# Scratch layout of q and k, pacing of the matrix comparison, and a bound in three steps, in a two-layer attention and Fourier kernel

## The chip, the cores and the metric

The kernel runs on one core of one Trainium2 chip. The metric is the device time of one execution in microseconds; the kernel before takes 2665.07 us (median of 3 runs, 2664.98 to 2665.43). Engines are called as the profile calls them: PE (matmul; PEld is its weight load), DVE (vector), ACT (scalar), POOL (GpSimd), SP (issues transfers). POOL and SP both start DMA transfers, each in the order of its own program.

## The reference

Two layers, each an attention block and a Fourier block on x of 2048 rows and 640 columns, 32 heads of 20 columns:

```
x = x + attention(layernorm(x))     # q, k, v = x @ wqkv;  softmax(q k^T / sqrt(20)) v;  @ wo
x = x + fourier(layernorm(x))       # a = x @ hid_re^T, b = x @ hid_im^T;  seq_re @ a - seq_im @ b
x = x + attention(layernorm(x))
x = x + fourier(layernorm(x))
```

The four matrices of the Fourier block are inputs. The kernel uses their mirror symmetry, and so compares their halves with each other once, in layer 0; a general path stands behind the comparison for matrices that aren't symmetric.

## The kernel before

**One layer.** A prologue normalizes and transposes x, and makes the first chunks of q and k and half of v. Then comes the attention, then the projection with wo, then the Fourier part. Most of the time is the attention: 8 groups of 4 heads, in a group 4 blocks of 512 queries (`qb`), in a block 16 chunks of 128 keys (`kc`): 512 steps a layer, numbered n. In a step `scores` (L469) makes four matmuls `psc<-stq,stk` and two exponentials `e<-psc` on ACT, and `values` (L480) the four matmuls `acc<-e,v` of a step or two earlier. After the last chunk of a block `finish` (L491) takes the sum `acc` out of PSUM with DVE (transpose `of`, division, transpose back `ot`, split `oh`), and POOL writes it out in eight transfers `o<-oh`, `o<-ot`. This finish of one block stands at kc 1 of the next.

**Exact halves.** A number f32 is split into a rounded part (high) and the rest (low). A score needs high times high, high times low, low times high. So the tile `stk` has, for each head, 60 rows of k (high, low, high) and `stq` 60 rows of q (high, high, low), and two rows of shift below them. `keep` (L208) writes both parts of a chunk of 128 columns of q or k and 512 rows of x to scratch in DRAM, `scr`, with a POOL transfer; `kload` (L433) and `qload` (L443) read them from there with SP transfers: for each head one of 40 rows and one of 20 rows, and for q one of the two rows of shift.

**Work beside the attention.** The other chunks of q, k and the second half of v are made during the attention, on PE, in the gaps of ACT (`work`, L347). For a chunk of 512 rows there are two pieces of matmuls `pqk<-xt,wqk`, two steps apart, then `keep` on DVE (`hl` twice, `sq`), two steps later the norms (`pn` on PE, `top` on DVE), and after four of these the weights of the next chunk are split on DVE (`wqk`, two instructions, `weights` L201). They all use one PSUM bank, `fill`: the next piece can start on PE only when `top` has read that bank and `wqk` is there. For v, `v<-pv` on DVE empties the bank. `due` (L541) says when a piece is due, `fill(n)` (L557) issues it, after the scores of its step. Work of this kind lasts to about step 350 in both layers.

**The comparison** (`Check`, L640, layer 0 only). 42 loads of 1 MB (two transfers `cq<-in_nat_seq_dram` of 512 KB) or less, and two small ones; POOL issues them, into two tiles that every load uses again. Behind each load stand four empty tasks and then the comparisons of it: the largest element (`ctop`), edges (`cedge`, small instructions), three or four pairs of a 128x512 subtraction (L688) and a reduction (L684). All tasks together are one list of 469. `begin(n)` (L574), ahead of the scores of step n, takes tasks from the list as long as fewer than 469 n / 490 are done; a load is held back when n modulo 64 is under 6 or over 54, that is around the change of a group. So the list can fall behind, and is then caught up within one step.

**The bound.** The scores of a group are shifted by a bound on them, from the norms. `bound(g + 1)` (L403) is called at kc 0 of the last block of group g: three small reductions on DVE, a power on POOL (L406), its product on DVE (L407), a copy to a row `sh` of 512 (L409), and an SP transfer to DRAM (L410), from where `qload` reads the two rows of shift. `sh`, the two tiles `of` and `ot` of `finish`, and `zeros` share one buffer (tag `ofsh`): the next to be written in it waits until the one before is read, by a transfer too.

**Loads around the change of a group.** In the last block of a group SP gets: at kc 0 the shift row, at kc 1 `kload` of the first half for heads 0 and 1 of the next group, at kc 4 its `qload`, at kc 9 and 11 two more `kload`; the last one comes at kc 0 of the new group and is used from its kc 8. There are five tiles for k and two pairs for q.

Of the kernel before, what the change touches and what calls it, by code (L numbers as in the profile page):

```python
# [5 lines left out]
F32 = mybir.dt.float32  # L6
# [28 lines left out]
def mha_fnet_kernel(ctx, tc, x_in, wqk, wv, wo, seq, hid, nat_seq, nat_hid, out):  # L35
# [123 lines left out]
    class Qkv:  # L159
        def __init__(s, L, src):  # L160
            s.L, s.src = L, src
            s.xn, s.xt, s.rs, s.v = {}, {}, {}, {}
            s.scr = {qk: dr.tile([2, D, S], F32, name=f"scr{qk}_{L}") for qk in "qk"}
            s.shift = {n: dr.tile([H, 2, c], F32, name=f"shift{n}_{L}") for n, c in (("b", 512), ("m", S))}
            s.n = 0
            s.made, s.raw = set(), {}
# [41 lines left out]
        def keep(s, p, c, tb, vector, room):  # L208

            hl = room("hl", [2, 512], F32R, "hl")  # L210
            sq = room("sq", [512], BF, "sq")
            h = hl[:, 0].bitcast(F32)
            if vector:
                split(hl[:, 0], hl[:, 1], p, vector)
                V.tensor_tensor(sq, h, h, op=OP.mult)
# [6 lines left out]
            G.dma_start(d[c * 128:(c + 1) * 128, :, tb * 512:(tb + 1) * 512], hl.bitcast(F32))  # L222
            return sq
# [38 lines left out]
        def prologue(s, vals, xt, fill, room, att):  # L262
# [36 lines left out]
            for tb in range(NB):  # L299
# [23 lines left out]
                if tb == 0:  # L323
                    att.qload(0, 0, None)
                elif tb == 1:
                    s.fetch(ND + 1)
                    for j in range(2):
                        att.kload(0, 0, j)
                elif tb == 2:
                    s.w1 = s.weights(s.fill("w", [2, ND, 128], F32R, "wqk"), ND + 1, True)  # L330
                    s.fetch(1)
                elif tb == NB - 1:
                    att.zeros(room)
                    s.bound(0, room)
                    att.qshift(0, 0)
                    for j in range(2):
                        att.kload(0, 1, j)
# [65 lines left out]
        def bound(s, g, room):  # L403

            r = s.bounds()
            G.tensor_tensor(r[:H, 3:4], r[:H, 2:3], half[:H, 0:1], op=OP.pow)  # L406
            V.tensor_scalar(r[:H, 3:4], r[:H, 3:4], -1.02, None, op0=OP.mult)  # L407
            sh = room("ofsh", [512], F32R, "sh")
            V.tensor_copy(sh[:H], r[:H, 3:4].to_broadcast([H, 512]))  # L409
            nc.sync.dma_start(s.shift["b"][4 * g:4 * g + 4, 0], sh[4 * g:4 * g + 4].bitcast(F32))  # L410

    class Attention:
# [17 lines left out]
        def kload(s, g, f, j):  # L433
# [3 lines left out]
            for i in range(2):  # L437
                r = slice((4 * g + 2 * j + i) * DH, (4 * g + 2 * j + i + 1) * DH)
                d = t[64 * i:64 * i + 60].bitcast(F32)
                nc.sync.dma_start(d[0:40], s.a.scr["k"][0:2, r, cols])  # L440
                nc.sync.dma_start(d[40:60], s.a.scr["k"][0, r, cols])

        def qload(s, g, qb, shift):  # L443
# [3 lines left out]
            for j in range(2):  # L447
                s.q[g, qb, j] = tiles[j]
                for i in range(2):
                    h = 4 * g + 2 * j + i  # L450
                    r = slice(h * DH, (h + 1) * DH)
                    d = tiles[j][64 * i:64 * i + 62].bitcast(F32)
                    nc.sync.dma_start(d[0:40], s.a.scr["q"][0:1, r, cols].to_broadcast([2, DH, 512]))
                    nc.sync.dma_start(d[40:60], s.a.scr["q"][1, r, cols])
                    if shift is not None:
# [78 lines left out]
        def run(s, done, project, check):  # L534

            work, tasks, later = s.a.work(), s.a.vweights(1, s.a.fill, pause=[lambda: None] * 2), list(check)
            s.work, s.blocks, s.after, s.rest, s.more = True, 0, None, 0, False

# [18 lines left out]
            def fill(n):  # L557
# [16 lines left out]
            def begin(n, g, qb, kc):  # L574
                if qb == NB - 1 and kc == 0 and g + 1 < H // 4:
                    c0, c1 = (g + 1) * 80 // 128, ((g + 2) * 80 - 1) // 128
                    need(n, c0, c1, ND + c0, ND + c1, *(["v"] if g + 1 >= 4 else []))
                    s.a.bound(g + 1, s.room)
                while later and (len(check) - len(later)) * 490 < n * len(check):
                    task = later.pop(0)  # L580
                    if isinstance(task, tuple):

                        if n % 64 < 6 or n % 64 > 54:
                            later.insert(0, task)
                            break
                        task = task[1]
                    task()

# [4 lines left out]

            s.sweep("b", begin, fill)
            assert not s.work and not later and not tasks, (len(later), len(tasks))
# [44 lines left out]
    class Check:  # L640
# [20 lines left out]
        def tasks(s):  # L661
# [6 lines left out]
            for i in range(2 * s.MID):  # L668
                out += [("load", lambda i=i: s.load(i))] + 4 * [lambda: None] + s.compare(i)
            for m in range(2):  # L670
                out += [("load", lambda m=m: s.middle(m))] + 4 * [lambda: None] + s.compare_middle(m)
            return out + [s.end, s.sum]
# [647 lines left out]
```

## Time and profile before

| | |
|---|---|
| time, median of 3 runs | 2665.07 us |
| the profiled execution: its time | 2668.6 us |
| its span, first to last instruction | 2666.7 us |
| mean granted clock of PE | 0.983 |
| busy: PE, ACT, DVE, POOL | 95%, 80%, 37%, 20% |
| exponentials `e<-psc`, ACT | 2048 in 1937.3 us of busy time |
| matmuls `acc<-e,v` / `psc<-stq,stk` | 1065.5 / 823.4 us of busy time |
| DMA, mean over the span | 99 GB/s |

The page gives for each engine the time in which it was busy, and for each group of instructions its number, the time of all, the mean of one, and how long the engine stood idle ahead of them and for whom. Matmuls overlap and their ends are modelled, so PE is called busy in times in which it could take more; whether the attention loses time is seen better from ACT, which has two exponentials to do in each step, and from the waits of PE. The two layers run the same program but for the comparison, which layer 0 alone has: a stage can be compared with itself.

### The profile page before, as it was taken

Reading aid. Unit: us, or ns where it says so; the run is one execution under the profiler, and the core shown is the slowest. Engines: PE = TensorE matmul, PEld = TensorE weight load, DVE = VectorE, ACT = ScalarE, POOL = GpSimd, SP = SyncE. Lnnn points to the kernel's source line nnn. Section 1 sums busy time; section 2 is a strip of 40 time slices with the busy share of each in tenths; the row PEclk is TensorE's granted clock in tenths of the full one; section 3 lists DMA queues with packets and bytes.
Section 4 is the critical chain, followed back from the end, with each engine's and each line's share of the span. In section 5 each row is a group of like instructions: output and inputs, shape, how many; then the busy total and the mean of one; then the engine's idle time right before and its main releaser. Section 6 shows DMA issues by size and latency. Waiting matters only on the chain. (4 is left out here: it accounts for less than half of the span.)

```text
span 2666.7 us, 43675 instructions
## 1 busy us (share of the span) xinstructions
PE 2542.7 (95%) x16350; PEld 1169.8 (44%) x16350; DVE 978.2 (37%) x2049; ACT 2136.3 (80%) x2429; POOL 525.0 (20%) x1062
## 2 busy tenths in 40 slices
PE   7999898989999999999969999999999999999997
PEld 6633343433333322228758444444433333222586
DVE  5354434435444444225553233211331211221265
ACT  5587697978899999994334888999889999999642
POOL 2122112112222212213241111111111111111133
PEclk9999999999999999999989999999999999999999
DMA  4333222223323322317263222111222111222264
GB/s 158 114 109 115 96 88 93 75 102 107 118 90 104 93 90 84 117 39 258 98 215 106 80 91 80 54 41 43 74 71 73 48 66 52 69 71 89 85 227 179
DMA packets 121820, 263.97 MB, mean 99 GB/s; under 512 B 24984, under 2 KB 49336, under 8 KB 121580
## 3 DMA queue, kind: packets, MB, share of 16 engines
q1 hardware_dynamic: 80684, 150.55, 16.7%
q0 software_dynamic: 40896, 110.34, 12.9%
q8 instruction: 137, 2.24, 0.4%
q14 instruction: 103, 0.84, 0.1%
HBM read 176.60 MB, written 84.16 MB: 98 GB/s over the span
## 5 line engine op out<-in xcount | busy, mean ns | idle before, releaser
L478 ACT ACTIVATE e<-psc 128x1024 f32<-128x1024 f32 x2048 | 1937.3, 1193 | 211.4 <-PE psc L475 175.8
L486 PE MATMUL acc<-e,v 128*32 128x512 f32 x8192 | 1065.5, 604 | 6.7 <-DVE of L493 6.6
L475 PE MATMUL psc<-stq,stk 62*128 62x512 f32 x4096 | 823.4, 465 | 8.0 <-DMA stk<-scrk 4.9
L475 PEld LDWEIGHTS psc<-stq,stk 62*128 62x128 f32 x4096 | 342.3, 184 | 850.9 <-ACT e L478 794.1
L486 PEld LDWEIGHTS acc<-e,v 128*32 128x32 f32 x8192 | 187.8, 108 | 369.2 <-issue 337.8
L126 PE MATMUL pqk<-xt,wqk 128*128 128x512 f32 x1200 | 317.5, 408 | 23.7 <-DVE top L228 13.4
L507 POOL DMA_DIRECT2D o<-oh x256 | 131.2, 518 | 803.5 <-DVE oh L502 774.9
L126 PEld LDWEIGHTS pqk<-xt,wqk 128*128 128x128 f32 x1200 | 217.0, 190 | 111.7 <-issue 39.6
L111 DVE CAST hl<-pqk 128x512 fp32r<-128x512 f32 x64 | 44.2, 691 | 517.9 <-PE pqk L126 516.7
L493 DVE STREAM_TRANSPOSE of<-acc 128x512 f32<-128x512 f32 x64 | 45.8, 716 | 376.5 <-PE acc L486 376.4
L126 PE MATMUL pv<-wv,xt 128*128 128x320 f32 x960 | 163.7, 322 | 11.7 <-DVE v L258 7.6
L126 PEld LDWEIGHTS pv<-wv,xt 128*128 128x128 f32 x960 | 144.6, 193 | 38.8 <-issue 24.6
L507 POOL DMA_DIRECT2D o<-ot x256 | 127.9, 506 | 5.4 <-DMA cq<-in_nat_seq_dram 4.6
L222 POOL DMA_DIRECT2D scrq<-hl x40 | 29.9, 748 | 440.7 <-DVE hl L114 311.4
L119 PE MATMUL py<-wo,o 128*128 128x320 f32 x320 | 100.9, 315 | 13.5 <-DVE xr L867 7.1
L684 DVE TENSOR_REDUCE far<-cq 128x1 f32<-128x512 f32 (+5 forms) x169 | 98.6, 584 | 5.7
L121 PE MATMUL py<-wo,o 128*128 128x320 f32 x320 | 100.2, 313 | 0.0
L120 PE MATMUL py<-wo,o 128*128 128x320 f32 x320 | 100.2, 313 | 0.0
L688 DVE TENSOR_TENSOR cq<-cq 128x512 f32<-128x512 f32 (+4 forms) x166 | 96.6, 582 | 7.4 <-DMA cq<-in_nat_seq_dram 7.3
L222 POOL DMA_DIRECT2D scrk<-hl x40 | 29.6, 740 | 352.6 <-DVE hl L114 337.4
L684 DVE TENSOR_REDUCE ctop<-cq 128x1 f32<-128x512 f32 (+2 forms) x44 | 27.4, 622 | 169.2 <-DMA cq<-in_nat_seq_dram 123.4
L258 DVE COPY v<-pv 128x320 f32<-128x320 f32 x32 | 15.7, 489 | 185.5 <-PE pv L126 185.5
(191 smaller groups left out, 1764.5 us busy)
## 6 DMA issues: line engine op xcount, KB each, us to landing
cq<-in_nat_seq_dram POOLq DMA_DIRECT2D x64, 512.0 KB, 5.4
scrq<-hl POOLq DMA_DIRECT2D x40, 512.0 KB, 3.2
scrk<-hl POOLq DMA_DIRECT2D x40, 512.0 KB, 5.0
stq<-scrq SPq DMA_DIRECT2D x256, 80.0 KB
stk<-scrk SPq DMA_DIRECT2D x128, 160.0 KB
o<-o SPq DMA_DIRECT2D x16, 1280.0 KB
stq<-scrq SPq DMA_DIRECT2D x256, 40.0 KB
stk<-scrk SPq DMA_DIRECT2D x128, 80.0 KB
```

What stands on the lines that cost most here:

```text
L119: PE.matmul(out_ap, ah, bh, start=start, stop=False)
L120: PE.matmul(out_ap, ah, bl, start=False, stop=False)
L121: PE.matmul(out_ap, al, bh, start=False, stop=stop)
L126: yield lambda i=i, j=j, k=k: PE.matmul(out_ap, a[i], b[j], start=dc == 0 and k == 0, stop=dc == ND - 1 and k == 2)
L222: G.dma_start(d[c * 128:(c + 1) * 128, :, tb * 512:(tb + 1) * 512], hl.bitcast(F32))
L475: PE.matmul(p[:, i], s.k[g, kc // 8, j][r, kc % 8 * 128:(kc % 8 + 1) * 128], s.q[g, qb, j][r], start=True, stop=True)
L478: A.activation(e, p, AF.Exp, scale=SCALE)
L486: PE.matmul(s.acc[32 * j:32 * j + 32], s.a.v[kc][:, v0:v0 + 32], s.e[n, j // 2][:, j % 2], start=kc == 0, stop=kc == NT - 1, skip_group_ch ...
L493: V.transpose(t0.rearrange("p b c -> p (b c)"), s.acc)
L507: G.dma_start(s.o[k, h * DH:(h + 1) * DH, qb * 512:(qb + 1) * 512], hl[k][32 * j:32 * j + DH])
L684: V.tensor_reduce(to, x, op=OP.max, axis=AX.X, apply_absolute_value=True)
L688: V.tensor_tensor(y, x, y, op=op)
```

## The change

There are four parts.

1. The scratch of q and k is laid out as column, part, row of x (`[D, 2, S]` in place of `[2, D, S]`): the high and low parts of a column follow each other. `kload` then reads 40 rows with one step between them, in the order high, low of each column, and `qload` reads each high row twice in a row; the order of rows in `stk` and `stq` changes in the same way in both, and the sum over them is the same.
2. The comparison has a function of its own, `compare(n)`, which is called after `fill(n)`, so behind the scores and the piece of work of its step. It takes two tasks a step at most, and after a load no task for five steps. The four empty tasks are gone (293 tasks in the list), and so is the ban around the change of a group.
3. `bound` is a generator in three steps: reductions and power at kc 0, product and copy to `sh` at kc 3, the transfer at kc 5.
4. `qload` for the next group is at kc 7 of the last block in place of kc 4; within a group it stays at kc 4.

```
-            s.scr = {qk: dr.tile([2, D, S], F32, name=f"scr{qk}_{L}") for qk in "qk"}
+            s.scr = {qk: dr.tile([D, 2, S], F32, name=f"scr{qk}_{L}") for qk in "qk"}
...
-            d = s.scr["qk"[k]].rearrange("j d t -> d j t")
-            G.dma_start(d[c * 128:(c + 1) * 128, :, tb * 512:(tb + 1) * 512], hl.bitcast(F32))
+            G.dma_start(s.scr["qk"[k]][c * 128:(c + 1) * 128, :, tb * 512:(tb + 1) * 512], hl.bitcast(F32))
...
             G.tensor_tensor(r[:H, 3:4], r[:H, 2:3], half[:H, 0:1], op=OP.pow)
+            yield
             V.tensor_scalar(r[:H, 3:4], r[:H, 3:4], -1.02, None, op0=OP.mult)
             sh = room("ofsh", [512], F32R, "sh")
             V.tensor_copy(sh[:H], r[:H, 3:4].to_broadcast([H, 512]))
+            yield
             nc.sync.dma_start(s.shift["b"][4 * g:4 * g + 4, 0], sh[4 * g:4 * g + 4].bitcast(F32))
+            yield
...
-                nc.sync.dma_start(d[0:40], s.a.scr["k"][0:2, r, cols])
-                nc.sync.dma_start(d[40:60], s.a.scr["k"][0, r, cols])
+                k = s.a.scr["k"][r, :, cols]
+                nc.sync.dma_start(d[0:40], k.rearrange("r j t -> (r j) t"))
+                nc.sync.dma_start(d[40:60], k[:, 0])
...
-                    nc.sync.dma_start(d[0:40], s.a.scr["q"][0:1, r, cols].to_broadcast([2, DH, 512]))
-                    nc.sync.dma_start(d[40:60], s.a.scr["q"][1, r, cols])
+                    q = s.a.scr["q"][r, :, cols]
+                    nc.sync.dma_start(d[0:40], q[:, 0:1].to_broadcast([DH, 2, 512]))
+                    nc.sync.dma_start(d[40:60], q[:, 1])
...
-                if kc == 4 and not (last and g == H // 4 - 1):
+                if kc == (7 if last else 4) and not (last and g == H // 4 - 1):
...
+            def compare(n):
+                for _ in range(2):
+                    if not later or n < s.landed or (len(check) - len(later)) * 490 >= n * len(check):
+                        break
+                    task = later.pop(0)
+                    if isinstance(task, tuple):
+                        s.landed = n + 5
+                        task = task[1]
+                    task()
...
-                    s.a.bound(g + 1, s.room)
-                while later and (len(check) - len(later)) * 490 < n * len(check):
-                    task = later.pop(0)
-                    if isinstance(task, tuple):
-                        if n % 64 < 6 or n % 64 > 54:
-                            later.insert(0, task)
-                            break
-                        task = task[1]
-                    task()
+                    s.shift = s.a.bound(g + 1, s.room)
+                if qb == NB - 1 and kc in (0, 3, 5) and g + 1 < H // 4:
+                    next(s.shift)
...
-                out += [("load", lambda i=i: s.load(i))] + 4 * [lambda: None] + s.compare(i)
+                out += [("load", lambda i=i: s.load(i))] + s.compare(i)
```

Three places in the order of instructions. The first is DVE around step 70 of layer 0, where the work beside the attention ends a chunk: `top<-pn` empties the bank, `wqk` are the weights of the next chunk, the rows on `cq` are comparisons of load 5. Before:

```order
L727 COPY cq<-cq 128x2
L688 TENSOR_TENSOR cq<-cq 128x512
L684 TENSOR_REDUCE far<-cq 128x1
L688 TENSOR_TENSOR cq<-cq 128x512
L684 TENSOR_REDUCE far<-cq 128x1
L228 TENSOR_REDUCE top<-pn 32x1
L111 CAST wqk<-wraw 128x640
L114 TENSOR_TENSOR wqk<-wraw,wqk 128x640
L688 TENSOR_TENSOR cq<-cq 128x512
```

and in the changed kernel:

```order
L697 TENSOR_REDUCE far<-cedge 128x1
L739 TENSOR_SCALAR cq<-cq 128x2
L740 COPY cq<-cq 128x2
L227 TENSOR_REDUCE top<-pn 32x1
L111 CAST wqk<-wraw 128x640
L114 TENSOR_TENSOR wqk<-wraw,wqk 128x640
L701 TENSOR_TENSOR cq<-cq 128x512
L697 TENSOR_REDUCE far<-cq 128x1
L701 TENSOR_TENSOR cq<-cq 128x512
```

Two pairs of subtraction and reduction have moved from ahead of `top` and `wqk` to behind them.

The second place is POOL at the change from group 0 to group 1, steps 49 to 68: the writes of the finished block (`o_95`), writes to scratch (`scrk_92`) and loads for the comparison (`cq`). Before:

```order
L507 DMA o_95<-ot 20x512 x4
L679 DMA cq<-in_nat_seq_dram 128x2x512 x2
L222 DMA scrk_92<-hl 128x2x512 x3
L507 DMA o_95<-oh 20x512 x4
L507 DMA o_95<-ot 20x512 x4
L222 DMA scrk_92<-hl 128x2x512
L679 DMA cq<-in_nat_seq_dram 128x2x512 x4
```

and now:

```order
L511 DMA o_95<-ot 20x512 x4
L221 DMA scrk_92<-hl 256x1x512
L692 DMA cq<-in_nat_seq_dram 128x2x512 x2
L221 DMA scrk_92<-hl 256x1x512 x2
L692 DMA cq<-in_nat_seq_dram 128x2x512 x2
L511 DMA o_95<-oh 20x512 x4
L511 DMA o_95<-ot 20x512 x4
L221 DMA scrk_92<-hl 256x1x512
```

Load 5 (the second `cq` row) has moved from behind the next block's writes and step 68's scratch write to ahead of the former, at step 64.

The third place is DVE in the last block of group 0, steps 48 to 52. Before, `sh` of the bound stands ahead of the finish of the block before (from `of<-acc` on):

```order
L400 TENSOR_TENSOR bound<-bound 32x1
L407 TENSOR_SCALAR bound<-bound 32x1
L409 CAST sh<-bound 32x512
L688 TENSOR_TENSOR cq<-cq 128x512
L684 TENSOR_REDUCE far<-cq 128x1
L688 TENSOR_TENSOR cq<-cq 128x256
L684 TENSOR_REDUCE far<-cq 128x1
L493 STREAM_TRANSPOSE of<-acc 128x512
```

Now it stands behind that finish (whose last instructions are the first three rows) and behind a `keep` (`hl`, `sq`), and ahead of the `top` of that `keep`:

```order
L504 STREAM_TRANSPOSE ot<-on 128x512
L506 CAST oh<-ot 128x512
L507 TENSOR_TENSOR ot<-ot,oh 128x512
L111 CAST hl<-pqk 128x512
L114 TENSOR_TENSOR hl<-pqk,hl 128x512
L215 TENSOR_TENSOR sq<-hl 128x512
L407 TENSOR_SCALAR bound<-bound 32x1
L409 CAST sh<-bound 32x512
L701 TENSOR_TENSOR cq<-cq 128x256
L697 TENSOR_REDUCE far<-cq 128x1
L227 TENSOR_REDUCE top<-pn 32x1
```

`sh` takes the buffer that `ot` held, so it has moved from a place where the transfers of an earlier block were the last readers to one where the four `o<-ot` of this finish are.

More of the change, by code (lines that the diff above doesn't have):

```diff
@@ L333, in prologue @@
                     att.zeros(room)
-                    s.bound(0, room)
+                    list(s.bound(0, room))
                     att.qshift(0, 0)
@@ L536, in run @@
             work, tasks, later = s.a.work(), s.a.vweights(1, s.a.fill, pause=[lambda: None] * 2), list(check)
-            s.work, s.blocks, s.after, s.rest, s.more = True, 0, None, 0, False
+            s.work, s.blocks, s.after, s.rest, s.more, s.landed = True, 0, None, 0, False, 0
             marks = ((0, 0), (44, 16), (236, 80), (364, 96), (512, 120))
@@ L592, in begin, with between @@
                     f()
-            s.sweep("b", begin, fill)
+            def between(n):
+                more = fill(n)
+                compare(n)
+                return more
+            s.sweep("b", begin, between)
             assert not s.work and not later and not tasks, (len(later), len(tasks))
@@ L668, in tasks @@
             for i in range(2 * s.MID):
-                out += [("load", lambda i=i: s.load(i))] + 4 * [lambda: None] + s.compare(i)
+                out += [("load", lambda i=i: s.load(i))] + s.compare(i)
             for m in range(2):
-                out += [("load", lambda m=m: s.middle(m))] + 4 * [lambda: None] + s.compare_middle(m)
+                out += [("load", lambda m=m: s.middle(m))] + s.compare_middle(m)
             return out + [s.end, s.sum]
```

## The prediction

> **What bounds the kernel now.** The two layers run the same attention, but only layer 0 compares matrices, so I lay them beside each other. The first view sums ACT's exponentials over the stretch of each group of 64 steps (stretch in us from the span's start, its length, ACT's busy time and number, granted clock of PE, DMA share, GB/s). Layer 0, then layer 1:
>
> ```profile
> 251.79:403.91 152.12, 123.88 (x129) 0.97 0.29 95
> ...
> 963.18:1080.42 117.24, 117.24 (x129) 1.00 0.29 86
> ...
> sum 1100.57, ACT 969.28; mean ACT 121.16
> ```
> ```profile
> 1604.76:1744.75 139.99, 123.84 (x128) 1.00 0.21 66
> ...
> 2270.51:2387.76 117.25, 117.25 (x129) 1.00 0.22 68
> ...
> sum 1048.12, ACT 968.02; mean ACT 121.00
> ```
>
> Layer 0 takes 1100.57 - 1048.12 = 52.45 us longer for the same exponentials. Group 6, in which comparisons run but no other work, takes 117.24 against 117.25 us: ACT is busy throughout, a step costs 117.25 / 64 = 1.83 us, and the comparison is free. Group 1, with work on PE beside it, takes 12.1 us longer. So the comparison costs only where something on PE waits for DVE. The next view gives what PE waited for (sum, times, longest), in the attention of layer 0 and then of layer 1:
>
> ```profile
> PE pqk L126 <- DVE top L228: 12.7, 3, 9.9
> PE pqk L126 <- DVE wqk L111: 9.2, 2, 8.5
> PE pv L126 <- DVE v L258: 7.6, 1, 7.6
> PE psc L475 <- DMA stk<-scrk: 4.9, 2, 3.7
> PE pn L227 <- DVE sq L215: 4.9, 3, 3.0
> PE acc L486 <- DVE of L493: 4.8, 11, 1.1
> PE psc L475 <- ACT e L478: 1.5, 3, 0.7
> ```
> ```profile
> PE acc L486 <- DVE of L493: 1.8, 10, 0.2
> PE psc L475 <- ACT e L478: 1.5, 3, 0.7
> PE pqk L126 <- DVE wqk L111: 0.8, 1, 0.8
> PE pqk L126 <- DVE top L228: 0.7, 2, 0.4
> PE pn L227 <- DVE sq L215: 0.5, 2, 0.3
> ```
>
> They sum to 45.6 and 5.3 us, a difference of 40.3. Layer 0 has four long waits (9.9, 8.5, 7.6, 3.7) and one of 3.0; nothing in layer 1 is over 0.8. The other 12 us are the clock. The stretches of layer 0's attention at half the granted clock that follow these waits, with PE's busy time first (the column ahead of 1.00 or 0.50 is POOL):
>
> ```profile
> 237.73:241.14 3.41, 3.41 (x15) 1.00 (x16) 3.34 (x7) 1.94 (x2) 0.00 (x0) 0.50 0.52 185
> 271.86:282.10 10.24, 4.54 (x12) 2.82 (x12) 8.56 (x22) 0.00 (x0) 1.33 (x2) 0.50 0.12 37
> 432.29:442.53 10.24, 6.50 (x28) 3.20 (x28) 6.45 (x12) 1.91 (x2) 1.43 (x2) 0.50 0.12 42
> 568.82:579.06 10.24, 4.22 (x10) 2.98 (x12) 6.06 (x16) 0.00 (x0) 1.42 (x2) 0.50 0.27 89
> 722.42:729.25 6.83, 6.63 (x25) 1.68 (x25) 5.29 (x9) 3.12 (x4) 0.72 (x1) 0.50 0.17 61
> ```
>
> PE works 25.3 us in them, which at full clock would take half: 12.6 us. With 40.3 that makes 52.9, near the measured 52.45. Layer 0's excess is explained, and it is all that the change can take back.
>
> **The pacing.** The list has 469 tasks over 490 steps, 0.96 a step. A load held back from about step 61 to step 70 leaves nine tasks due at once: the load, four empty ones, and four comparisons of that very load. So the comparison waits for a transfer issued in the same step, and `top` and `wqk` stand behind it (first place of the order). The timeline shows it:
>
> ```profile
> 264.90 1.45 POOL L679 DMA_DIRECT2D cq<-in_nat_seq_dram  x2
> 271.79 0.69 DVE L684 TENSOR_REDUCE ctop<-cq 128x1 f32<-128x512 f32 x1 [7.33 <-DMA cq<-in_nat_seq_dram]
> 273.79 0.69 DVE L688 TENSOR_TENSOR cq<-cq 128x512 f32<-128x512 f32 x1
> 274.51 0.69 DVE L684 TENSOR_REDUCE far<-cq 128x1 f32<-128x512 f32 x1
> 275.12 0.68 DVE L688 TENSOR_TENSOR cq<-cq 128x512 f32<-128x512 f32 x1
> 277.56 3.78 PE L126 MATMUL pqk<-xt,wqk 128*128 128x512 f32 x8 [8.47 <-DVE wqk L111]
> ```
>
> DVE sits 7.33 us on the transfer, then does comparisons, a pair every 1.33 us; PE waits 8.47 us for `wqk`. The two lines of pacing give the same pattern wherever the ban ends: steps 70, 134, 198, 262, 326, which are the places of layer 0's excess.
>
> In the changed kernel no comparison comes sooner than five steps after its load: 5 x 1.83 = 9.2 us at least, against 271.79 - 264.90 = 6.9 us here. The four long waits should go with their clock. What remains I count from the new order. At step 208 a pair now stands between a `keep` and the next `wqk`, at the place where layer 1 already waits 0.8 us, so its 1.33 us are exposed: **1.3 us**. Around step 84 the order holds about what it held: of the shorter `top` waits I keep **0.8**. The waits of `acc` for `of` come from pairs just ahead of a finish; a pair or two still stands there in a dozen blocks: I keep 4.8 - 1.8 = **3.0**.
>
> **The bound: an added wait.** `sh` at kc 3 now takes the buffer of `ot`, whose four writes have only been issued (third place). In layer 1, first change of group, from DVE, POOL and PE, and the landing of all `o<-ot` writes:
>
> ```profile
> 1567.06 0.41 DVE L409 CAST sh<-bound 32x512 fp32r<-32x512 f32 x1
> ...
> 1571.52 0.72 DVE L493 STREAM_TRANSPOSE of<-acc 128x512 f32<-128x512 f32 x1 [4.05 <-PE acc L486]
> ...
> 1577.79 0.68 DVE L228 TENSOR_REDUCE top<-pn 32x1 f32<-32x512 f32 x1 [0.47 <-PE pn L227]
> ```
> ```profile
> 1577.41 2.00 POOL L507 DMA_DIRECT2D o<-ot  x4
> ```
> ```profile
> 1580.86 2.12 PE L126 MATMUL pqk<-xt,wqk 128*128 128x512 f32 x8
> ```
> ```profile
> DMA to landing us min/median/max: 1.8/3.5/7.5
> ```
>
> The last of the four starts at 1577.41 + 1.5 = 1578.9; with the median it lands at 1582.4. DVE holds at `sh` until then, needs 0.41 us for it, and `top` follows with 0.68: 1583.5. PE wants the bank at 1580.86, so it waits **2.7 us**; in layer 0 a pair on 256 of the 512 columns stands ahead of `top` too, between half and all of 1.33, say 0.85: **3.55 us**. With the shortest and longest landing these would be 1.0 to 6.7 in layer 1; I take the median. At the other changes of group nothing on PE stands behind `sh` before it is done: after group 1 and 2 the work is v, whose next bank is needed four and more steps later, then there is no piece until kc 12. Before, the same buffer was waited for at kc 0, fifteen steps after its writes; that costs nothing and goes.
>
> **The loads.** While only 40-row loads of k run (700 to 703 us), SP's queue takes 12.6% of 16 DMA engines, two of them; in the 0.3 us of a 20-row load beside one, 61.8%, ten:
>
> ```profile
> q1 hardware_dynamic: 39, 0.16, 12.6%
> ```
> ```profile
> q1 hardware_dynamic: 13, 0.05, 61.8%
> ```
>
> The order prints the old 40-row source with a dimension ahead (`40x1x1024`) and the new one plain (`40x1024`), as the 20-row load always was. So I expect the 160 KB to spread over ten engines. The two late `stk` (4.9 us above) go with it; in layer 1 nobody waits for these loads, so nothing more is gained there. What this covers is the later `qload`: `sh` is done 1582.8 - 1571.5 = 11.3 us, 6.2 steps, after the finish of kc 1 began (the row of `of`), so at kc 8, and q and one `kload` have 8 steps, 14.6 us, left. A write to scratch is now issued as 256 rows; were its 748 ns doubled, POOL, which stands idle 440 us ahead of those writes, would hide it:
>
> ```profile
> L222 POOL DMA_DIRECT2D scrq<-hl x40 | 29.9, 748 | 440.7 <-DVE hl L114 311.4
> ```
>
> The Trainium skill, "DMA: Bandwidth & Descriptors", section "Why a DMA increments its semaphore by 16 and not by 1", says that a transfer runs on the largest number of engines up to 16 that divides the outermost dimension on both sides. By that the old 40-row loads get 2 (the 12.6% agrees), the new ones of k and of q 10; for q, whose printed shape does not change, no run here shows it. With that rule q is as quick as k and the sum below stands; without it the third case below becomes likelier.
>
> **Sum.** Left over: 1.3 + 0.8 + 3.0 + 2.7 + 3.55 = 11.4 us. Gain: 52.45 - 11.4 = 41.0. The profiled execution took 2668.6 us (span 2666.7), so 2627.6; the median of the runs shown is 3.5 us lower, and I forecast **2624 us**, with 2616 to 2633 for other landings of `ot`, a half-clock stretch after the 3.55 us (half of 3.41: 1.7), and other waits of `acc`.
>
> **Rivals.**
>
> *Nothing new waits:* the `ot` writes land early, since the two crowded engines are freed, and the pairs stay hidden. Then only some of the 52.45 stay: 2612 to 2616. For it: landings as short as 1.8. Against: the median, and the 1.3 us at step 208.
>
> *The pairs crowd DVE:* two tasks in a step are 2.7 us against 1.83 to 2.5 of a step, and in the new order some 13 `keep` cycles have a pair or more before the next piece. If each exposes one, 13 x 1.33 = 17 us more: 2641. Against: layer 0's short waits already hold such cycles at a fraction of that.
>
> *The loads come late (slower):* if 40-row loads stay on two engines, q and k can miss the first step of a group. The place is SP's queue in the last block:
>
> ```profile
> 677.08 0.61 SPq L453 DMA_DIRECT2D stq<-scrq  x1
> ...
> 693.28 0.22 SPq L456 DMA_DIRECT2D stq<-shiftb  x1
> ```
>
> The twelve issues of q took 16.4 us there. With them 14.6 us are overrun; four issues of k (2.4, at 0.61) and 3.0 us for the 160 KB that the 12.6% row moved in its window make 7.2 us late, at 14 changes of group 101 us: some 2725. It decides against the change from 41 / 14 = 2.9 us on. If the loads spread, the sixteen issues alone take at most 16 x 0.61 = 9.8 us, and with 3.5 us to land they fit, with 1.3 us to spare.
>
> **How the numbers follow.** Forecast 0.70; nothing new waits 0.09; pairs crowd DVE 0.14; loads late 0.07, of which 0.04 lose more than the rest gains. The range from 2613 to 2640 holds the first three nearly whole. A measurement of this kernel can tell about 0.2%, 5 us, from no change. Faster by more: 0.94; within: 0.02; slower: 0.04.
>
> **What would show it.** Right: layer 0's attention some 9 us above layer 1's, which is 1 to 3 us above 1048; no wait of PE over 4 us in it; waits of `pqk` for `top` near step 54 in both layers, with DVE standing at `sh` for the DMA `o<-ot`; SP's queue at more than half of 16 engines under k loads; no half clock but perhaps after step 54. Wrong: PE waiting for `stq` or `stk` at the first step of a group, or DVE idle for `cq` ahead of a `keep`'s `top`.

## The result, and the profile after

The changed kernel takes 2623.84 us, the median of four runs (2622.28 to 2624.82), beside 2665.03 (2664.98 to 2665.43): a ratio of 0.9845, 95% interval 0.9828 to 0.9862. Against this 2624 was forecast. The profiled execution took 2624.82 us, with a span of 2623.0 against 2666.7. The span is cut at the exponentials:

| stretch, us | before | after | less |
|---|---|---|---|
| attention of layer 0 | 1100.57 | 1057.59 | 42.98 |
| between the two attentions | 259.22 | 257.84 | 1.38 |
| attention of layer 1 | 1048.12 | 1049.08 | -0.96 |
| ahead of the first and behind the second | 258.8 | 258.5 | 0.3 |

The gain lies in layer 0's attention, as forecast; the 1.38 us between the attentions was not. The groups of 64 steps, by the view that sums ACT's exponentials over each (stretch, its length, ACT's busy time and number, PE's granted clock, DMA share, GB/s), layer 0 and then layer 1:

```profile
249.10:390.54 141.44, 124.10 (x128) 1.00 0.34 109
...
sum 1057.59, ACT 968.51; mean ACT 121.06
```
```profile
1561.11:1701.10 139.99, 123.85 (x128) 1.00 0.21 66
...
sum 1049.08, ACT 968.02; mean ACT 121.00
```

Group 1 was 12.1 us longer in layer 0 than in layer 1, and is now 1.45 longer. Its granted clock was 0.97 and is 1.00. What PE still waits for (sum, times, longest), in the attention of layer 0 and of layer 1:

```profile
PE acc L490 <- DVE of L497: 6.6, 12, 2.3
PE pqk L126 <- DVE top L227: 3.5, 3, 2.8
```
```profile
PE acc L490 <- DVE of L497: 1.8, 10, 0.2
PE pqk L126 <- DVE top L227: 1.7, 3, 1.0
```

The waits of 9.9, 8.5 and 7.6 us for `top`, `wqk` and `v` are gone, and so is `stk`. The longest left is 2.8 us. Of the five stretches at half clock one is left, with PE at work throughout (the 1.00-or-0.50 column is the granted clock):

```profile
224.09:227.50 3.41, 3.41 (x10) 2.28 (x10) 0.00 (x0) 0.00 (x0) 0.73 (x2) 0.50 0.83 253
```

With the four rows that follow in both (1.5, 0.8, 0.3 and 0.3) the waits sum to 13.0 and 6.4 us. Their difference, 6.6, and half of 3.41 make 8.3, near the 8.5 by which layer 0 is now longer than layer 1. So no more than 0.2 us of the difference is left unexplained.

The timeline at steps 64 to 70, where before DVE stood 7.33 us for a load and PE 8.47 us for `wqk`:

```profile
249.17 1.50 POOL L692 DMA_DIRECT2D cq<-in_nat_seq_dram  x2 [0.69 <-DVE far L697]
...
261.68 0.68 DVE L697 TENSOR_REDUCE ctop<-cq 128x1 f32<-128x512 f32 x1
...
263.25 0.68 DVE L227 TENSOR_REDUCE top<-pn 32x1 f32<-32x512 f32 x1 [0.20 <-PE pn L226]
```

`ctop`, the first comparison of the load, starts 12.5 us after its issue and has no bracket: DVE did not stand idle for the transfer. `top` now waits 0.20 us for PE, no longer the other way round. Elsewhere DVE still stands for a load: 2 us or more seven times up to step 350 (16 times before), 4.2 to 7.5 us each. PE waits for it at none of these places.

The added wait is where the prediction put it, at step 54 of both layers. First layer 0, DVE and then PE:

```profile
221.84 0.42 DVE L409 CAST sh<-bound 32x512 fp32r<-32x512 f32 x1 [4.54 <-DMA o<-ot]
...
222.96 0.67 DVE L227 TENSOR_REDUCE top<-pn 32x1 f32<-32x512 f32 x1
```
```profile
223.68 3.46 PE L126 MATMUL pqk<-xt,wqk 128*128 128x512 f32 x8 [2.82 <-DVE top L227]
```

Then layer 1: the four writes from `ot` on POOL, DVE, and the landing of all such writes.

```profile
1532.74 2.00 POOL L511 DMA_DIRECT2D o<-ot  x4
```
```profile
1536.15 0.42 DVE L409 CAST sh<-bound 32x512 fp32r<-32x512 f32 x1 [3.46 <-DMA o<-ot]
1536.50 0.67 DVE L227 TENSOR_REDUCE top<-pn 32x1 f32<-32x512 f32 x1
```
```profile
DMA to landing us min/median/max: 1.8/1.8/5.4
```

The last write starts at 1532.74 + 1.5 = 1534.24, and `sh` may go 1.9 us later, where the forecast used 3.5. PE's wait is then 1.0 us (the longest in layer 1's row for `top`), not 2.7. In layer 0 the same writes took longer, about what was forecast: the last starts at 216.95 + 1.5 = 218.45, and `sh` goes 3.4 us later.

```profile
216.95 1.99 POOL L511 DMA_DIRECT2D o<-ot  x4
```

At the 14 changes of group DVE stands between 3.5 and 5.9 us for `o<-ot` ahead of `sh`; only at the first of each layer, at step 54, does a wait of PE over 0.5 us come of it, as the prediction said.

### The profile page after: what moved, and what is told of

Read it like the earlier page. It is cut to its first block, busy times and chain, and to the rows that moved or that the text cites. A ratio compares the mean times of both kernels' runs of the same rounds, so it can differ in the third digit from the quotient of the medians.

```text
span 2623.0 us, 43686 instructions
## 1 busy us (share of the span) xinstructions
PE 2531.0 (96%) x16350; PEld 1164.4 (44%) x16350; DVE 976.3 (37%) x2049; ACT 2135.4 (81%) x2429; POOL 522.6 (20%) x1062
## 5 line engine op out<-in xcount | busy, mean ns | idle before, releaser
L257 DVE COPY v<-pv 128x320 f32<-128x320 f32 x32 | 15.7, 490 | 182.2 <-PE pv L126 182.2
L227 DVE TENSOR_REDUCE top<-pn 32x1 f32<-32x512 f32 x80 | 53.5, 675 | 56.5 <-PE pn L226 56.5
```

The costliest lines, as they stand in the source:

```text
L227: V.tensor_reduce(s.top[:H, c // ND, c % ND, tb:tb + 1], p, op=OP.max, axis=AX.X)
```

## The experiments

Times are medians, and ratios are to the kernel before on the same chip (2664.82, 2667.85 and 2666.34 us there). The last two columns are the attentions of layer 0 and 1 in the profiled execution, to be read against 1100.6 and 1048.1 before and 1057.6 and 1049.1 after. A "+" at a step is the time of that step in layer 0 over that of the same step of layer 1. What the texts below call off or back is of layer 0's attention, unless they name the time.

| run | kernel | us | ratio, 95% | layer 0 | layer 1 |
|---|---|---|---|---|---|
| e1_pacing | before, new pacing | 2632.22 | 0.9878 [0.9862, 0.9895] | 1063.4 | 1048.1 |
| e2_layout | before, new layout | 2651.49 | 0.9944 [0.9928, 0.9961] | 1084.9 | 1048.1 |
| e11_no_ban | before, no ban | 2643.18 | 0.9920 [0.9904, 0.9936] | 1072.1 | 1048.2 |
| e7_no_gap | changed, no five steps | 2631.35 | 0.9861 [0.9845, 0.9877] | 1064.4 | 1049.3 |
| e4_narrow | changed, old layout | 2668.27 | 1.0014 [1.0004, 1.0024] | 1093.4 | 1059.3 |
| e10_narrow_one | e4, bound in one step | 2631.79 | 0.9875 [0.9857, 0.9892] | 1068.2 | 1048.2 |
| e3_bound_one | changed, bound in one step | 2624.18 | 0.9845 [0.9829, 0.9861] | 1057.3 | 1048.1 |
| e6_own_buffer | changed, `sh` in a buffer of its own | 2620.07 | 0.9821 [0.9804, 0.9837] | 1053.3 | 1048.1 |
| e8_behind | changed, comparison last in its step | 2621.28 | 0.9824 [0.9808, 0.9841] | 1054.9 | 1049.3 |
| e9_best | e6 and e8 together | 2619.99 | 0.9821 [0.9804, 0.9837] | 1054.4 | 1048.2 |
| e12_as_is | the changed kernel again | 2625.28 | 0.9850 [0.9835, 0.9864] | 1057.6 | 1049.3 |
| e13_own_again | e6 again | 2620.28 | 0.9829 [0.9815, 0.9842] | 1054.6 | 1048.2 |

### The pacing alone (e1)

```
-                while later and (len(check) - len(later)) * 490 < n * len(check):
-                    task = later.pop(0)
-                    if isinstance(task, tuple):
-                        if n % 64 < 6 or n % 64 > 54:
...
+            def compare(n):
+                for _ in range(2):
+                    if not later or n < s.landed or (len(check) - len(later)) * 490 >= n * len(check):
...
-                out += [("load", lambda i=i: s.load(i))] + 4 * [lambda: None] + s.compare(i)
+                out += [("load", lambda i=i: s.load(i))] + s.compare(i)
```

> The kernel before with the pacing alone (two tasks a step, five steps behind a load, behind the work of the step); scratch, bound and qload as before. Theory A (the long waits of PE come from comparisons standing ahead of their own transfer): the three waits of 7.6 to 9.9 us and the one of 3.0 go with their half clock, the two late k loads (4.9 us) stay; layer 0's attention 1060 to 1066 us against 1100.6, time about 2628. Theory B (the two crowded DMA engines make the comparison's data late, so the layout is needed too): data still land later than five steps in places, waits of PE over 3 us remain, layer 0's attention 1070 to 1085, time 2635 to 2650.

Layer 0's attention loses 37.2 of the 43.0 us that the whole change takes from it. What stays, by the view of PE's waits in it:

```profile
PE acc L486 <- DVE of L493: 8.1, 12, 3.6
PE psc L475 <- DMA stk<-scrk: 3.6, 2, 3.4
```

The second row is the late `stk` that the new layout was to end: with the half clock behind it, it costs 5.0 us at step 328. The first is larger than in the changed kernel (8.1 against 6.6): step 242 costs 4.5 here and 2.0 there.

### The layout alone (e2)

```
-            s.scr = {qk: dr.tile([2, D, S], F32, name=f"scr{qk}_{L}") for qk in "qk"}
+            s.scr = {qk: dr.tile([D, 2, S], F32, name=f"scr{qk}_{L}") for qk in "qk"}
...
-                nc.sync.dma_start(d[0:40], s.a.scr["k"][0:2, r, cols])
-                nc.sync.dma_start(d[40:60], s.a.scr["k"][0, r, cols])
+                k = s.a.scr["k"][r, :, cols]
+                nc.sync.dma_start(d[0:40], k.rearrange("r j t -> (r j) t"))
+                nc.sync.dma_start(d[40:60], k[:, 0])
...
-                    nc.sync.dma_start(d[0:40], s.a.scr["q"][0:1, r, cols].to_broadcast([2, DH, 512]))
-                    nc.sync.dma_start(d[40:60], s.a.scr["q"][1, r, cols])
+                    q = s.a.scr["q"][r, :, cols]
+                    nc.sync.dma_start(d[0:40], q[:, 0:1].to_broadcast([DH, 2, 512]))
+                    nc.sync.dma_start(d[40:60], q[:, 1])
```

> The kernel before with the new layout of q and k alone. Theory A: the late k loads go (4.9 us of waits and a half-clock stretch of 6.8 us), the waits behind comparisons stay at 7 us or more each; layer 0's attention 1088 to 1095, time 2652 to 2660. Theory B: the comparison's data come soon enough once the engines are free, most of the 52 us go; layer 0's attention 1060 to 1075, time 2625 to 2640.

It takes 15.7 us off by itself, and 13.3 off the time, a little more than expected. The long waits for DVE stay, and no row for `stk` is left:

```profile
PE pqk L126 <- DVE top L227: 11.9, 3, 9.1
PE pqk L126 <- DVE wqk L111: 9.1, 2, 8.4
```

With `v` (6.2) these are steps 72 (+10.4), 140 (+7.6) and 200 (+11.1). Gone are the excess at steps 264 (6.5 us in the kernel before, with the late `stk`) and 58 (4.4). 37.2 and 15.7 sum to 52.9, and e3 (below), which has both, takes 43.3 off: the parts share 9.6 us. The excess at steps 58 and 264 goes with either.

### Which part of the pacing (e11 and e7)

In the kernel before, with its list, only the ban on loads goes:

```
                     if isinstance(task, tuple):
-                        if n % 64 < 6 or n % 64 > 54:
-                            later.insert(0, task)
-                            break
                         task = task[1]
```

> The kernel before without the ban on loads around the change of a group, and nothing else: no backlog can build up, and the four empty tasks keep a load about four steps ahead of its first comparison. Theory (the backlog behind the ban makes the bursts, and the bursts the long waits): most of what the pacing alone gave comes from this, layer 0's attention 1062 to 1072, time 2630 to 2640. Rival (the limit of two tasks and the place behind the work are needed): layer 0's attention over 1080, time over 2646.

In the changed kernel, only the five steps go:

```
-                        s.landed = n + 5
+                        s.landed = n
```

> The changed kernel without the five steps between a load and its first comparison; two tasks a step at most stay, and the loads are spread as before. Theory A (what costs is a comparison ahead of its own transfer): each of some 25 loads beside the other work makes DVE wait about 7 us, PE waits of 2 to 6 us come back at many of them, layer 0's attention 1075 to 1110, time 2640 to 2675. Rival (what costs is the burst of many comparisons in one step, which the limit of two takes away): layer 0's attention stays under 1062, time under 2630.

Without the ban nothing heaps up, and the three waits of 7.6 to 9.9 us for `top`, `wqk` and `v` are gone; 28.4 us come off. The time, 2643.18, misses the 2630 to 2640 that were expected. What is left in layer 0's attention begins with late loads, which cost more than before (8.2 against 4.9 us):

```profile
PE psc L475 <- DMA stk<-scrk: 8.2, 3, 4.3
```

Without the five steps, but with at most two tasks a step and no ban, only 6.8 us come back (1064.4 - 1057.6), of which 4.9 at step 90. Theory A had 1075 to 1110 for this attention, and its rival under 1062:

```profile
PE pqk L126 <- DVE top L227: 6.5, 4, 3.1
```

So it was the heap behind the ban that made the waits of 8 to 10 us. The distance to the load is worth 6.8 of 43. Yet DVE stands for a load in e7 more often than in the kernel before: 2 us or more 21 times up to step 350, 2.8 to 7.5 us each, against 16 times. Only five steps (19, 55, 90, 99 and 100) are over 0.5 us longer than in the changed kernel. A wait of DVE for a load thus costs little by itself; it is dear where many comparisons follow it and `top`, `wqk` or `v` stand behind them. No run keeps the ban and limits the tasks of a step, so what the limit of two is worth by itself is not shown.

### The layout under the changed kernel (e4 and e10)

e4 is the changed kernel with the old layout and its loads (the diff of e2, reversed). e10 is e4 with the bound in one step, at kc 0:

```
-                    s.shift = s.a.bound(g + 1, s.room)
-                if qb == NB - 1 and kc in (0, 3, 5) and g + 1 < H // 4:
-                    next(s.shift)
+                    list(s.a.bound(g + 1, s.room))
```

> The changed kernel with the old layout of q and k, so 40-row loads on two engines, with the later shift and qload. Theory C of the prediction (the loads come late): PE waits for stq or stk at the first step of groups, 3 us or more at most of 14 changes of group, time 2660 to 2720. Theory D (the loads have room even on two engines): at most the late stk at kc 8 of layer 0 comes back, time 2624 to 2634.

> The changed kernel with the old layout (40-row loads on two engines) and the bound in one step at kc 0; qload stays at kc 7. Theory (what makes the narrow loads late is the shift, which waits for sh, which waits for the ot writes, with q and k queued behind it on SP): with sh early the loads are in time again as in the run with pacing alone; layer 0's attention 1062 to 1066 us, layer 1's 1048, time 2629 to 2635. Rival (the later place of qload makes them late): the stalls at the first steps of groups stay, layer 0's attention about 1090, layer 1's about 1059, time about 2665.

The gain is gone, and layer 1, which no comparison touches, is 11.2 us longer than before. PE's waits, layer 0 and then layer 1 of e4, and layer 0 of e10:

```profile
PE psc L478 <- DMA stk<-scrk: 24.0, 10, 4.3
```
```profile
PE psc L478 <- DMA stk<-scrk: 6.4, 5, 2.0
```
```profile
PE psc L478 <- DMA stk<-scrk: 5.1, 3, 3.1
```

The slower rival of the prediction is thus real, at changes of group (step 128 +2.6, 192 +7.6) and eight steps behind such a change (264 +5.3, 328 +5.5), but its time is 44.4 us over the changed kernel and not 101. The rival had 7.2 us at each of the 14 changes. Step by step against the changed kernel, ten of them lose between 1.6 and 8.6 us, up to 20 steps behind the change counted, and four lose nothing. Which of the two moves is it, the bound's or q's? SP's queue ahead of step 192, in e4 and then in e10 (start, length, issue):

```profile
503.64 0.24 SPq L412 DMA_DIRECT2D shiftb<-sh  x1
503.99 0.61 SPq L456 DMA_DIRECT2D stq<-scrq  x1
...
513.63 0.61 SPq L443 DMA_DIRECT2D stk<-scrk  x1
...
519.83 3.21 SPq L444 DMA_DIRECT2D stk<-scrk  x1
```
```profile
488.06 0.24 SPq L412 DMA_DIRECT2D shiftb<-sh  x1
...
490.85 0.61 SPq L456 DMA_DIRECT2D stq<-scrq  x1
```

Both have q at kc 7. In e10 the transfer `shiftb` is out early, and q and k behind it have 13 us more (490.85 against 503.99). In e4 it waits for `sh`, and `sh` for the writes from `ot`:

```profile
503.19 0.42 DVE L410 CAST sh<-bound 32x512 fp32r<-32x512 f32 x1 [3.81 <-DMA o<-ot]
```

Everything on the queue waits behind it, and then the loads of q and those of k follow each other closely: one issue takes 3.21 us. So the three steps of the bound need the new layout. The place of q by itself does not: e10 differs from e1 in nothing else, and its time is the same (ratio 0.9875 beside 0.9878). In the profiled executions its layer 0 is 4.8 us longer than that of e1, and 2 us over what was expected; 3.0 of the 4.8 are at step 72, behind a late `stk`. At step 192 of the changed kernel the same queue is past q at the same time (513.64 against 513.63), and an issue of k holds it for 0.27 us in place of 0.61:

```profile
502.30 0.24 SPq L411 DMA_DIRECT2D shiftb<-sh  x1
...
513.64 0.27 SPq L443 DMA_DIRECT2D stk<-scrk  x1
```

### The bound: in one step (e3), and with a buffer of its own (e6)

e3 is the changed kernel with the edit of e10. e6 keeps the three steps and gives `sh` a small buffer, 128 columns that the transfer reads four times:

```
-            sh = room("ofsh", [512], F32R, "sh")
-            V.tensor_copy(sh[:H], r[:H, 3:4].to_broadcast([H, 512]))
+            c = 128 if g else 512
+            sh = room("shown" if g else "ofsh", [c], F32R, "sh")
+            V.tensor_copy(sh[:H], r[:H, 3:4].to_broadcast([H, c]))
...
-            nc.sync.dma_start(s.shift["b"][4 * g:4 * g + 4, 0], sh[4 * g:4 * g + 4].bitcast(F32))
+            row = s.shift["b"][4 * g:4 * g + 4, 0].rearrange("h (a c) -> h a c", c=c)
+            nc.sync.dma_start(row, sh[4 * g:4 * g + 4, None].bitcast(F32).to_broadcast([4, 512 // c, c]))
```

> The changed kernel with the bound in one step at kc 0 again (qload stays at kc 7). Theory (the copy to sh waits for the ot writes whose buffer it takes): the stall at step 54 goes in both layers, 4.9 us in layer 0 and 1.4 in layer 1; time about 2617.5, layer 0's attention about 1052.7, layer 1's 1047.7. Rival (those stalls have another cause, such as the work beside the attention at this place): step 54 stays at 7.0 and 3.6 us, time 2624.

> The changed kernel with a small buffer of its own for sh (128 columns, which the transfer reads four times), the bound still in three steps. Theory (the copy to sh waits for the ot writes whose buffer it takes): the stalls at step 54 go, 4.9 us in layer 0 and 1.4 in layer 1, and nothing new comes at steps 52 and 242, since the reductions stay spread: layer 0's attention about 1053, layer 1's 1048, time about 2618. Rival (step 54 stalls for the place of the work, or for the power on POOL): 7.0 and 3.6 us stay there, time 2624.

Both take the stall at step 54 away in both layers. But e3 was to reach 2617.5 and did not: at step 242 `of` comes later, and its timeline shows why.

```profile
635.48 0.14 DVE L407 TENSOR_SCALAR bound<-bound 32x1 f32<-32x1 f32 x1 [0.75 <-POOL bound L405]
635.69 0.42 DVE L409 CAST sh<-bound 32x512 fp32r<-32x512 f32 x1
...
639.26 0.71 DVE L497 STREAM_TRANSPOSE of<-acc 128x512 f32<-128x512 f32 x1
```
```profile
PE acc L490 <- DVE of L497: 8.1, 12, 3.6
```

DVE stands 0.75 us for POOL's power and 0.42 for `sh`, ahead of the finish, where comparisons crowd it already; PE then waits up to 3.6 us there (2.3 in the changed kernel), and step 242 is +4.4 in place of +2.0, with 3.41 us at half clock behind the wait. Step 52 is +1.4. In the changed kernel these instructions come later and meet `ot`. In e6 they do neither. PE's waits for `of` in its layer 0 are the 6.6 us of the changed kernel, and those for `top` have gone from 3.5 us to

```profile
PE pqk L126 <- DVE top L227: 0.7, 2, 0.4
```

Its attention is 4.3 us shorter in layer 0 and 0.9 in layer 1 than that of the changed kernel, 5.2 in all for the two terms that the prediction had put at 6.25.

### The comparison behind the finish (e8, e9)

The leftover waits are those of `acc` for `of`, with a pair ahead of it. In e8 the comparison is called last in a step; e9 has e6's buffer as well.

```
-                if fill(n) and n >= 2 and kc != 1 and n + 1 < len(s.steps):
-                    continue
-                while done < n - 1:
-                    s.values(done)
-                    done += 1
+                if not (fill(n) and n >= 2 and kc != 1 and n + 1 < len(s.steps)):
+                    while done < n - 1:
+                        s.values(done)
+                        done += 1
+                behind(n)
```

> The changed kernel with the comparison's tasks of a step issued behind the values and the finish of that step, where they now stand ahead of them. Theory (waits of acc come from pairs just ahead of a finish): the excess at steps 82, 210, 242 and 274 (1.3, 0.7, 2.0, 0.9 us) goes, step 54 stays; layer 0's attention about 1053, time about 2619. Rival (the finish waits for something else, or the pairs delay the next keep or top instead): 1057 and 2624 stay.

> Own buffer for sh and the comparison behind the finish, together. If both theories hold: layer 0's attention within 2 us of layer 1's, 1048 to 1050, and time 2612 to 2615. If the stalls only move: 2618 or more.

In both the waits of `acc` fall by half, and others rise. PE's waits in layer 0 of e8:

```profile
PE pqk L126 <- DVE top L227: 4.5, 3, 2.3
PE acc L490 <- DVE of L497: 3.1, 11, 0.9
PE pn L226 <- DVE bound L407: 1.6, 1, 1.6
```

The pair now stands ahead of `top` at step 84 (+1.9 in e8) and of the bound at step 52 (+1.3). e9 was to come to 2612 to 2615; it is e6's time. In e6, e8 and e9 layer 0 stays 5 to 6 us longer than layer 1: in the places tried, the exposed work of DVE moved and did not go.

### The two versions again (e12, e13)

> The changed kernel once more, beside the version with a buffer of its own for sh on the same chip: 2622 to 2625 us.

> The changed kernel with a buffer of its own for sh once more: 4 to 6 us under the changed kernel on the same chip, as its attention was 4.3 us shorter in layer 0 and 0.9 in layer 1; if the first difference was the chip's, the two agree within 2 us.

Five runs each on one chip: the changed kernel 2623.51 to 2629.24, with its own buffer 2618.22 to 2624.22. The medians differ by 5.0 us, about what can be told here, and the ranges touch; the first run of e6 differed from the changed kernel by 3.8, and the stall that goes is to be seen in each trace (step 54 takes 6.9 us in layer 0 and 3.6 in layer 1 of e12, and 2.6 in both of e13). So with `sh` in a buffer of its own the kernel is faster than the changed one with some likelihood, by 4 to 5 us. e8 and e9 can't be told from it.

## Why the prediction came out right, point by point

**Layer 1 as the measure of layer 0.** Right. It bounded the gain at 52.45 us and named what was to go; 42.98 went.

**The heap behind the ban.** Right in mechanism, and shown by e11: without those three lines the three long waits for DVE are gone. (The fourth, for `stk`, goes with the layout: e2.) The reason given second, that the five steps keep a comparison off its own load, is the smaller part (e7: 6.8 us). Nor are the five steps the 9.2 us at least that the prediction made of them. At step 90 of the changed kernel POOL comes late to the load, behind a write to scratch that waited for `hl`, and DVE is at `ctop` 1.9 us after the issue (310.97 - 4.18 - 304.92):

```profile
304.34 0.71 POOL L221 DMA_DIRECT2D scrq<-hl  x1 [5.92 <-DVE hl L114]
304.92 1.45 POOL L692 DMA_DIRECT2D cq<-in_nat_seq_dram  x2
```
```profile
310.97 0.69 DVE L697 TENSOR_REDUCE ctop<-cq 128x1 f32<-128x512 f32 x1 [4.18 <-DMA cq<-in_nat_seq_dram]
```

PE does not wait here: the `top` that it needs next stands ahead of `ctop`.

**What is left over.** Forecast 11.4 us, measured 9.5 in layer 0 (1057.59 - 1048.12) and 1.0 in layer 1. The sum is right to 1 us, the terms are not; that their errors cancel is luck:

| term | forecast | measured |
|---|---|---|
| pair ahead of `wqk`, step 208 to 212 | 1.3 | 0 at `wqk`; 0.7 at `of`, counted in the third row |
| shorter `top` waits, step 84 | 0.8 | 0 |
| `acc` for `of` | 3.0 | 4.9 (steps 82, 210, 242, 274: 1.28, 0.69, 2.01, 0.95) |
| `sh` behind `ot`, layer 1 | 2.7 | 1.0 |
| the same, layer 0 | 3.55 | 4.4 |

The first two were read from the order alone. The pair of step 208 does stand there, but it stands ahead of the finish too: `of` is later for it, and PE loses 0.7 us at step 210. When PE comes to `wqk` it is late by as much itself, and waits no longer than in layer 1 (step 212 takes 3.79 us, and 3.78 there). Step 84 is no longer than in layer 1. The third was mis-sized: the largest part is one place, step 242, where two pairs stand ahead of the finish in a row, and `of` begins only when the second is done:

```profile
639.55 0.68 DVE L701 TENSOR_TENSOR cq<-cq 128x512 f32<-128x512 f32 x1
640.27 0.69 DVE L697 TENSOR_REDUCE far<-cq 128x1 f32<-128x512 f32 x1
640.87 0.70 DVE L497 STREAM_TRANSPOSE of<-acc 128x512 f32<-128x512 f32 x1
```

The fourth took 3.5 us for the landing of `ot`, the median of a kernel with the old layout; with the new one the median is 1.8 (below), and it was 1.9 at this place. The prediction named this possibility, in its first rival, and gave it too little weight. In layer 0 the landing was 3.4 us, near the forecast. There PE's wait was 2.82 us, under the 3.55, and half of the 3.41 us at half clock came on top: 4.5, against the 4.4 us by which step 54 is longer than in the kernel before (6.99 and 2.57). That clock stood in the range, not in the term.

The sum was made for the profiled execution and then lowered by 3.5 us. The profiled executions differ by 43.8 us and the medians by 41.2, where 41.0 was forecast. That the median was met to 0.2 us is luck too.

**The loads.** Right: `stk` is waited for by nobody, and SP's queue alone takes 59.9% of the 16 engines while k is loaded (1545.2 to 1546.0), and 51.0% in 0.8 us of q (1538.4 to 1539.2), each with its 20-row load beside it:

```profile
q1 hardware_dynamic: 58, 0.18, 59.9%
```
```profile
q1 hardware_dynamic: 75, 0.12, 51.0%
```

A 20-row load took 61.8% already before, so the first row alone does not settle it for k. Over four such pairs (1543.8 to 1549.4) the queue moves 0.87 MB in 5.6 us, and the four 20-row loads are only 0.33 of that. The rest, 0.54 MB, would have taken 10 us at the old rate of the 40-row loads, 0.16 MB in 3 us:

```profile
q1 hardware_dynamic: 313, 0.87, 53.1%
```

Whether q's 40 rows spread had been left open. The second row has 60 of its 75 packets from a 40-row and a 20-row load. At the rate of the old loads the 80 KB of the 40 rows alone would take 1.5 us. The rule of the Trainium skill ("DMA: Bandwidth & Descriptors", section "Why a DMA increments its semaphore by 16 and not by 1"), by which such a load gets ten engines (the largest number up to 16 that divides 20 rows at the source and 40, or 20, at the destination), agrees with this row. As cover for the later transfer of the shift the layout is worth more than alone: by the times, 44.4 us from e4 to the changed kernel, and 13.3 in e2.

**Rivals.** That nothing new waits was half true in layer 1. That pairs crowd DVE at 13 places was not: four places, 4.9 us. That late loads decide was excluded by the layout, and e4 shows what it excluded.

**The bound in three steps and the later q** earn nothing here: e3, without the first, takes the same time, and e10, which is e1 with the second, takes e1's time (on the old layout; no run has the new one with q at kc 4). The three steps move DVE's work out of step 242 and into a wait for `ot`; with the wait taken away (e6) the move is worth 3.9 us of attention over e3.

**Left open.** The 1.38 us between the attentions: no part of the change touches it, and over the runs of the table it lies between 255.8 and 258.6 us, also in those that are the kernel before with one edit, so it may be no effect of the change. Why stalls at DVE's crowded steps move rather than vanish was followed at three places (54, 84, 242) and not further.

## What to carry to other kernels

Where two parts of a program run the same work and only one has something beside it, their difference by step, with waits and half clock added up, says what there is to win and where; a price read from the order of instructions alone says only where to look. A rule that holds work back makes a heap where it ends: without the ban 28.4 us were saved, although late loads cost 3.3 us more. Whether a limit on how fast the heap comes out would have served as well, with the ban kept, no run shows. When a step is moved, ask which buffer it takes and whose transfer still reads that, and try a buffer of its own before moving it again.

## What the hardware showed that was not expected

- Transfers of another queue landed later while loads ran on two engines. Three pairs of kernels differ in the layout alone, and the median landing of the writes from `ot`, which POOL issues, is 3.5 and 1.8 us (before, e2), 2.7 and 1.8 (e4, the changed kernel), 3.7 and 1.8 (e10, e3). Over all, it is 2.7 to 4.0 us in the five kernels with the old loads and 1.8 to 2.0 in the nine with the new. For the writes to `scrk`, whose own layout changes too, it is 4.6 to 5.2 and 3.3 to 3.5. That the two crowded engines are the reason is argued from this, and not tried apart from the layout.
- The issue of a 40-row k load holds SP for 0.61 us with the old layout, on two engines, and for 0.27 with the new. It is not a matter of the engines alone: that of a 40-row q load went from 0.61 to 0.77 us. An issue took up to 3.21 us in e4 where loads were still under way.
- A wait of PE of 2.82 us was followed by 3.41 us at half clock, as one of 3.0 us was before; one of 1.0 us in layer 1 was not. In between, the length does not decide: the wait for `of` at step 242 is 2.25 us in the changed kernel and in e13, and is followed by 3.41 us at half clock in e13 alone, where the step is +3.0 and not +2.0. The Trainium skill ("TensorE: Matmul & The Clock Gate", section "Why this matters for your kernels") says to keep gaps under about 3 us; here a gap of 2.25 us lost the clock once. The wait and the stretch at half clock in e13 (the column of 0.50 is the granted clock):

```profile
637.28 1.80 PE L492 MATMUL acc<-e,v 128*32 128x512 f32 x8 [2.25 <-DVE of L499]
```
```profile
637.48:640.89 3.41, 3.41 (x16) 0.70 (x12) 3.24 (x8) 0.99 (x2) 0.94 (x2) 0.50 0.02 5
```
